# Attention of a fused kernel: transposes, values and outputs an iteration later, GpSimd's work in another order

## The chip, the core and the metric

One core of a Trainium2 chip runs the whole program. The metric is the device time of one execution in microseconds (us). The engines are TensorE (PE in the rows, PEld for its weight loads), VectorE (DVE), ScalarE (ACT), GpSimd (POOL) and SyncE (SP), which here issues every transfer (DMA). Each engine takes its own instructions strictly in the order in which they were written; semaphores make one wait for another.

## What is computed

Local attention with block summaries, then two gated layers. For 16 heads (2 batches of 8), 768 positions and 64 channels, a row sees the positions nearer than 16 and, as 24 further keys, the maxima of `k` over blocks of 32; their values are the block means of `v`:

```python
k_sum = k.reshape(B, H, nb, block, D).max(axis=3)
v_sum = v.reshape(B, H, nb, block, D).mean(axis=3)
scores_l = scale * np.matmul(q, k.transpose(0, 1, 3, 2))
scores_s = scale * np.einsum('bhsd,bhnd->bhsn', q, k_sum) + np.log(block)
a = softmax over [scores_l where |i - j| < 16, scores_s]
x = (a @ concat(v, v_sum)) as 1536 tokens x 512
x = (h * cos(h)) @ w_out            with h = x @ w_in       (2048 wide)
x = (h * tanh(softplus(h))) @ w2_out  with h = x @ w2_in    (2048 wide)
```

Inputs are float32 or, for the weights, float64 that is read as pairs of words and narrowed on the chip.

## The kernel before

The attention goes over 24 steps. A step is a pair of heads and a third of its positions: pair n has the steps 3n, 3n + 1 and 3n + 2. Iteration i of the loop in `attention` works on several steps at once: it computes the scores of step i, the softmax of step i - 1, the transposes of the probabilities of step i - 2 (`probsT`, from `pn` by products with `ident`, copied from PSUM to `pt`), the value products of step i - 3 (`pv`), and the outputs of step i - 4 (`evac`: a rounded high part `xh` by ScalarE and the rest `xl` by VectorE). Beside them it prepares pairs to come: `k` and `q` are transposed on TensorE; ScalarE copies `k` into `kx`; VectorE takes the block maxima `ks` and scales `q` into `qt`; GpSimd copies `qt` into the two halves of `qb`. A softmax step is a row maximum `mx` on VectorE, four exponentials `pb` on ScalarE with their sums, sum and reciprocal `rs` on VectorE, and the multiply `pn` on GpSimd (the phase "norm").

The functions don't issue instructions at once. Each puts them into a named phase with `at(phase, ...)`, and `flush()` at the end of an iteration writes them out phase by phase in the order of the tuple `ORDER`. So `ORDER` sets what stands ahead of what on every engine within an iteration. Loads (`load`, `load_v`, `load_vb`) are written when `plan(i, ...)` comes to them, ahead of everything that `flush` writes; the transfers of the phase "misc" are written last.

The block means of `v` come in two ways. For a pair n with 2n < `MADE` they are made on TensorE: `prep_vm` multiplies the pair's values by a matrix `means`, twelve products into a bank, and ScalarE copies the result into `vm`. For the other pairs GpSimd adds up 32 rows in `block_sums` over a tile `vb` (two groups of `HPG` heads), scales the sums into `vs`, and SP moves them from `vs` to `vm` by small transfers; GpSimd then copies the first half of `vm` to a third place. In both ways `prep_vs` sends `vm` into the value tile `vw` of the pair by two transfers (`vw<-vm`), and the pair's value products need them. There are three value tiles, two of each of `kn`, `qn`, `vm`.

Between the attention's instructions stands the start of the weights: at given iterations `wload` fetches a chunk of `w_in`, `wnarrow` turns it to float32 (one op on ScalarE, three on VectorE: L131, L135, L138, L141) and `wsplit` makes a high and a low part (ScalarE L149, GpSimd L152). In the last iterations the first three blocks of up-projection products (`up`, L188) stand in the phase "fill". After the loop `layers` runs the two gated layers; its first gate begins with L556 on ScalarE and L557 on VectorE.

Of the kernel before, what the change touches and what calls it, by code (L numbers as in the profile page):

```python
# [21 lines left out]
def kernel(  # L22
# [11 lines left out]
    nc = tc.nc  # L34
# [18 lines left out]
    GAP = NB // 2  # L53
# [139 lines left out]
    HPG = 5  # L193
# [4 lines left out]
    def attention(filler):  # L198
        with ExitStack() as es:
# [49 lines left out]
            def build_means():  # L249

                nc.gpsimd.memset(means, 1.0 / BLK)
                for pattern, base, step in (
# [9 lines left out]
            ORDER = ("sc", "xh", "sums", "max", "tr", "tp", "ev", "qev", "pv", "pth", "fill", "qbd", "kmax", "rec", "exp",  # L262
                     "xl", "norm", "gap", "misc")
            todo = {o: [] for o in ORDER}

            def at(phase, fn, *a, **kw):
                todo[phase].append(lambda: fn(*a, **kw))  # L267
# [45 lines left out]
            def prep_vm(n):  # L313
                vm = VM[n] = p2.tile([GAP, 3, 2, D], F32, tag="vm", name="vm")
                if 2 * n >= MADE:
                    for e in range(2):
                        i = 2 * n + e - MADE
                        src = VS[i // HPG][NB * (i % HPG):NB * (i % HPG) + NB]
                        for h in range(2):
                            at("misc", nc.sync.dma_start, out=vm[:, h, e, :], in_=src[GAP * h:GAP * h + GAP])  # L320
                    at("misc", nc.gpsimd.tensor_copy, vm[:, 2], vm[:, 0])
                    return
# [71 lines left out]
            plan(0, prep_vm, 0)  # L394
            plan(1, prep_vs, 0)
# [9 lines left out]
            for n in range(1, NP):  # L405
                plan(3 * n + 1 if 2 * n < MADE else 3 * n, prep_vm, n)
                plan(3 * n + 2 if 2 * n < MADE else 3 * n + 1, prep_vs, n)
                if n > 2:
                    plan(3 * n - 3, load_v, n)
            for g in range(2):  # L410
                plan((2, 9)[g], load_vb, g)
                for c in range(9):
                    plan((4, 11)[g] + c // 2, block_sums, g, c)
# [99 lines left out]
            for i in range(NS + 5):  # L513
                if i >= 4 and i - 4 < NS:
                    evac(i - 4)
# [4 lines left out]
                if 2 <= i < NS + 2:  # L520
                    probsT(i - 2)
                for f in PREP.get(i, ()):
                    f()
                if 3 <= i < NS + 3:
                    pv(i - 3)
# [374 lines left out]
    NS = len(STEPS)  # L900
# [5 lines left out]
    for c, (t0, t1) in enumerate(((7, 10), (9, 12), (13, 16), (15, 18))):  # L906
        at_step(t0, wload, 0, 0, c)
        for part in range(4):
            at_step(t1 + part // 2, wnarrow, 0, 0, c, part)
        at_step(t1 + 2, wsplit, 0, 0, c)  # L910
    at_step(19, wload, 0, 0, 4)
    at_step(21, wload, 0, 0, 5)
# [39 lines left out]
```

## Time and profile before

| what | us |
|---|---|
| median of 3 runs | 654.89 (653.13 to 655.21) |
| the profiled execution | 655.26, its span 653.5 |
| TensorE busy in the span | 616.2 (94%) |
| VectorE busy | 500.9 (77%) |
| ScalarE busy | 333.5 (51%) |
| GpSimd busy | 86.1 (13%) |

The span is the time from the first to the last instruction. The engines' shares are means over parts with different limits: the attention takes the first fifth of the span, the two layers the rest. A row of the timeline shows the start, the duration, engine and line, the operation with output <- inputs and shapes, the number of instructions merged into the row, and in brackets how long the engine was idle before it and what ended that. L267 is the line on which the phases are recorded, so the attention's instructions all carry it and are told apart by their tiles.

### The profile page before, as it was taken

What the parts mean: (1) busy time and instruction counts of PE and PEld (TensorE: products, weight loads), DVE (VectorE), ACT (ScalarE), POOL (GpSimd) and SP (SyncE); (2) the same over time, 40 slices, a digit from 0 to 9 for tenths busy, and PEclk for the clock granted to TensorE, in tenths of its full rate; (3) what the DMA queues carried; (4) which work ended last, traced back from release to release, by engine and by line L of the source; (5) the groups of instructions that cost most, each with busy time, mean ns of one, the idle gap of its engine ahead of it and who ended that gap; (6) DMA issues with size and microseconds to landing.
All of it is one profiled execution on the core that took longest, in us unless ns stands there. A gap on an engine that the chain in (4) does not pass through costs nothing.

```text
span 653.5 us, 8522 instructions
## 1 busy us (share of the span) xinstructions
PE 616.2 (94%) x3004; PEld 515.2 (79%) x3004; DVE 500.9 (77%) x879; ACT 333.5 (51%) x733; POOL 86.1 (13%) x165
## 2 busy tenths in 40 slices
PE   7894877986999999999999999999999999999997
PEld 6784766864888888888888888888888888888886
DVE  4466666398778988888888986977888888888653
ACT  3575676575555644444445545654344444444230
POOL 5483766100000000000000223000000000000000
PEclk9998788997999999999999999999999999999999
DMA  9896844012112212212121210212122222120004
GB/s 186 169 176 151 165 100 107 6 65 96 65 66 96 98 65 65 65 64 66 64 65 66 64 33 0 66 64 66 65 64 65 64 66 81 49 96 33 2 16 178
DMA packets 58665, 51.26 MB, mean 78 GB/s; under 512 B 45326, under 2 KB 46734, under 8 KB 58382
## 3 DMA queue, kind: packets, MB, share of 16 engines
q1 hardware_dynamic: 58622, 50.71, 28.2%
q8 instruction: 24, 0.39, 0.3%
q14 instruction: 19, 0.16, 0.1%
HBM read 46.31 MB, written 3.15 MB: 76 GB/s over the span
## 4 chain that ended last, share of the span: by engine, by line
PE 83%; DVE 6%; POOL 3%; DMA 3%; issue 1%; ACT 1%; SPq 1%; POOLq 0%; ACTq 0%; DVEq 0%
PE bank L709 20%; PE bank L580 20%; PE bank L694 19%; PE bank L188 18%; PE bank L267 7%; POOL pn L267 1%; DMA vb<-in_v_dram 1%; DMA vm<-vs 1%; DVE wx L138 1%; POOL qb L267 1%; DVE wx L141 1%; DVE r L558 1%; POOL ws L152 1%; DVE r L557 1%; DMA vw<-in_v_dram 1%
## 5 line engine op out<-in xcount | busy, mean ns | idle before, releaser
L580 PE MATMUL bank<-gh,ws 128*128 128x512 f32 x384 | 126.7, 392 | 4.9 <-ACT ws L149 4.2
L188 PE MATMUL bank<-xh,ws 128*128 128x512 f32 x384 | 128.1, 395 | 2.0 <-DVE gg L564 1.9
L709 PE MATMUL bank<-ws,gh 128*128 128x512 f32 (+1 forms) x388 | 118.4, 387 | 0.0
L694 PE MATMUL bank<-xh,ws 128*128 128x512 f32 x272 | 91.1, 389 | 0.0
L580 PEld LDWEIGHTS bank<-gh,ws 128*128 128x128 f32 x384 | 72.3, 188 | 21.7 <-ACT ws L149 4.9
L188 PEld LDWEIGHTS bank<-xh,ws 128*128 128x128 f32 x384 | 73.1, 190 | 18.5 <-DVE gg L564 3.3
L709 PEld LDWEIGHTS bank<-ws,gh 128*128 128x128 f32 x388 | 72.6, 188 | 14.8
L556 ACT ACTIVATE n<-bank,b_quarter 128x512 int32<-128x512 f32 x48 | 32.9, 686 | 87.6 <-PE bank L188 87.6
L188 PE MATMUL bank<-xl,ws 128*128 128x512 f32 x192 | 75.6, 394 | 0.0
L709 PE MATMUL bank<-ws,gl 128*128 128x512 f32 (+1 forms) x194 | 75.0, 387 | 0.0
L580 PE MATMUL bank<-gl,ws 128*128 128x512 f32 x192 | 74.9, 390 | 0.0
L149 ACT CAST ws<-wx 128x512 fp32r<-128x512 f32 x64 | 39.6, 620 | 51.5 <-DVE wx L141 51.5
L694 PEld LDWEIGHTS bank<-xh,ws 128*128 128x128 f32 x272 | 51.1, 188 | 10.6
L665 DVE TENSOR_TENSOR gl<-gg,gh 128x512 fp32r<-128x512 f32 x48 | 34.0, 707 | 30.2 <-ACT gh L664 30.2
L721 DVE TENSOR_TENSOR acc<-acc,bank 128x512 f32<-128x512 f32 (+1 forms) x71 | 47.4, 673 | 8.5 <-PE bank L709 8.5
L557 DVE SCALAR_TENSOR_TENSOR r<-n,bank 128x512 f32<-128x512 int32 x48 | 32.8, 684 | 27.2 <-ACT n L556 27.2
L694 PE MATMUL bank<-xl,ws 128*128 128x512 f32 x136 | 52.9, 389 | 0.0
L595 POOL TENSOR_TENSOR xl<-acc,xh 128x512 fp32r<-128x512 f32 x10 | 14.0, 1416 | 261.4 <-ACT xh L593 261.4
L138 DVE SCALAR_TENSOR_TENSOR wx<-wst,wx 128x512 int32<-128x512 int32 x64 | 45.6, 712 | 2.2
L141 DVE SCALAR_TENSOR_TENSOR wx<-wst,wx 128x512 int32<-128x512 int32 x64 | 44.4, 694 | 1.8
L152 DVE TENSOR_TENSOR ws<-wx,ws 128x512 fp32r<-128x512 f32 x60 | 42.1, 703 | 4.8 <-ACT ws L149 4.1
L671 ACT ACTIVATE gg<-gg 128x512 f32<-128x512 f32 x28 | 17.7, 633 | 51.2 <-DVE gg L670 51.2
(110 smaller groups left out, 1062.2 us busy)
## 6 DMA issues: line engine op xcount, KB each, us to landing
wst<-in_moe_w_in_dram SPq DMA_DIRECT2D x32, 512.0 KB
wst<-in_moe_w_out_dram SPq DMA_DIRECT2D x32, 512.0 KB
kn<-in_k_dram SPq DMA_DIRECT2D x16, 192.0 KB
qn<-in_q_dram SPq DMA_DIRECT2D x16, 192.0 KB
vw<-in_v_dram SPq DMA_DIRECT2D x16, 192.0 KB
out_dram<-acc SPq DMA_DIRECT2D x11, 256.0 KB
vb<-in_v_dram SPq DMA_DIRECT2D x2, 960.0 KB
vw<-in_v_dram SPq DMA_DIRECT2D x32, 41.2 KB
```

Source lines behind the costliest of these rows:

```text
L138: nc.vector.scalar_tensor_tensor(out=xi, in0=word[:, :, 0], scalar=29, in1=xi, op0=ALU.logical_shift_right, op1=ALU.bitwise_or)
L141: nc.vector.scalar_tensor_tensor(out=xi, in0=word[:, :, 1], scalar=-2 ** 31, in1=xi, op0=ALU.bitwise_and, op1=ALU.bitwise_or)
L149: nc.scalar.copy(hi, x)
L152: eng.tensor_tensor(out=lo, in0=x, in1=hi.bitcast(F32), op=ALU.subtract)
L188: nc.tensor.matmul(ps, lhsT=SLOT[4 * (g % 2) + a][:, 512 * c + 128 * f:512 * c + 128 * f + 128], rhs=X[e][:, c, TB * j:TB * j + TB], start ...
L267: todo[phase].append(lambda: fn(*a, **kw))
L557: nc.vector.scalar_tensor_tensor(out=r, in0=n, scalar=-C1, in1=h, op0=ALU.mult, op1=ALU.add)
L580: nc.tensor.matmul(ps, lhsT=x, rhs=y, start=(n == 0), stop=(n == len(mm) - 1))
L665: later.append(lambda: nc.vector.tensor_tensor(out=lo, in0=g, in1=hi.bitcast(F32), op=ALU.subtract))
L694: nc.tensor.matmul(ps, lhsT=u, rhs=v, start=start and n == 0, stop=stop and n == len(mm) - 1)
L709: nc.tensor.matmul(ps, lhsT=x, rhs=y, start=(n == 0 and (h == 0 or not stay)), stop=(n == len(mm) - 1 and (h == NH - 1 or not stay)))
L721: nc.vector.tensor_tensor(out=acc, in0=acc, in1=ps, op=ALU.add)
```

## The change

Transposes, values and outputs of a step come one iteration later (i - 3, i - 4, i - 5), and the loop's last iteration now has work. `ORDER` is another: the reciprocals ("rec") come right behind the maxima and the evictions, and the multiply ("norm") ahead of the copies into `qb`, of the weights' part and of the sums, which now come last but two. `HPG` is 4 instead of 5, so that four pairs instead of three have their means from products, and the groups of sums have 96 rows instead of 120. The third part of `vm` comes by transfers, six in place of four, not by a copy on GpSimd. The means of pair 0 are made in iterations 2 and 3 instead of 0 and 1; values are loaded one iteration later; `vb` is loaded at 1 and 12 instead of 2 and 9 and its sums spread over more iterations; the first weight chunks come one or two iterations later.

```diff
-    HPG = 5
+    HPG = 4
...
-            ORDER = ("sc", "xh", "sums", "max", "tr", "tp", "ev", "qev", "pv", "pth", "fill", "qbd", "kmax", "rec", "exp",
-                     "xl", "norm", "gap", "misc")
+            ORDER = ("sc", "xh", "max", "tr", "tp", "ev", "rec", "pth", "pv", "qev", "norm", "kmax", "qbd", "fill", "exp",
+                     "xl", "sums", "gap", "misc")
...
-                        for h in range(2):
-                            at("misc", nc.sync.dma_start, out=vm[:, h, e, :], in_=src[GAP * h:GAP * h + GAP])
-                    at("misc", nc.gpsimd.tensor_copy, vm[:, 2], vm[:, 0])
+                        for h in range(3):
+                            r0 = GAP * (h % 2)
+                            at("misc", nc.sync.dma_start, out=vm[:, h, e, :], in_=src[r0:r0 + GAP])
...
-            plan(0, prep_vm, 0)
-            plan(1, prep_vs, 0)
+            plan(2, prep_vm, 0)
+            plan(3, prep_vs, 0)
...
-                    plan(3 * n - 3, load_v, n)
-            for g in range(2):
-                plan((2, 9)[g], load_vb, g)
-                for c in range(9):
-                    plan((4, 11)[g] + c // 2, block_sums, g, c)
+                    plan(3 * n - 2, load_v, n)
+            for g, at0, steps in ((0, 1, (4, 5, 6, 7, 8, 9, 10, 10, 11)), (1, 12, (14, 14, 15, 15, 16, 16, 17, 17, 18))):
+                plan(at0, load_vb, g)
+                for c, i in enumerate(steps):
+                    plan(i, block_sums, g, c)
...
-                if i >= 4 and i - 4 < NS:
-                    evac(i - 4)
+                if 5 <= i < NS + 5:
+                    evac(i - 5)
...
-                if 2 <= i < NS + 2:
-                    probsT(i - 2)
+                if 3 <= i < NS + 3:
+                    probsT(i - 3)
...
-                if 3 <= i < NS + 3:
-                    pv(i - 3)
+                if 4 <= i < NS + 4:
+                    pv(i - 4)
...
-    for c, (t0, t1) in enumerate(((7, 10), (9, 12), (13, 16), (15, 18))):
+    for c, (t0, t1) in enumerate(((8, 12), (10, 14), (15, 17), (17, 19))):
...
-        at_step(t1 + 2, wsplit, 0, 0, c)
-    at_step(19, wload, 0, 0, 4)
-    at_step(21, wload, 0, 0, 5)
+        at_step(t1 + 3, wsplit, 0, 0, c)
+    at_step(20, wload, 0, 0, 4)
+    at_step(22, wload, 0, 0, 5)
```

SP, at the end of the loads of the first three pairs: before, the two transfers of pair 0's means into its value tile (`vw0<-vm`) stand ahead of the sums' rows `vb` and of pair 3's `kn` and `qn`.

```order
L291 DMA vw2_110<-in_v_dram 15x11x64
L267 DMA vw0_108<-vm_262 12x6x256 x2
L300 DMA vb_366<-in_v_dram 120x2048
L280 DMA kn_419<-in_k_dram 128x6x64 x2
L280 DMA qn_422<-in_q_dram 128x6x64 x2
L280 DMA kn_538<-in_k_dram 128x6x64 x2
```

The same place now:

```order
L291 DMA vw2_110<-in_v_dram 15x11x64
L300 DMA vb_307<-in_v_dram 96x2048
L280 DMA kn_411<-in_k_dram 128x6x64 x2
L280 DMA qn_414<-in_q_dram 128x6x64 x2
L267 DMA vw0_108<-vm_350 12x6x256 x2
L280 DMA kn_523<-in_k_dram 128x6x64 x2
```

The pair of transfers has moved past five others.

GpSimd, two iterations in the middle with sums over `vb` and the weights' subtraction (`ws`, L152): before, the multiply `pn` comes last of these in its iteration.

```order
L267 TENSOR_TENSOR vb_764<-vb_764 120x256 x2
L152 TENSOR_TENSOR ws1_84<-wx_838,ws0_83 128x512
L267 COPY qb1_107<-qt_914 64x4x64 x2
L267 TENSOR_TENSOR pn_912<-pb_858,rs_911 128x472
L267 COPY vm_918<-vm_918 12x128
L267 TENSOR_TENSOR vb_764<-vb_764 120x256 x2
L267 COPY qb1_107<-qt_978 64x4x64 x2
L267 TENSOR_TENSOR pn_976<-pb_908,rs_975 128x472
```

Such iterations now:

```order
L267 TENSOR_TENSOR pn_1061<-pb_1006,rs_1060 128x472
L267 COPY qb0_106<-qt_1063 64x4x64 x2
L152 TENSOR_TENSOR ws1_84<-wx_936,ws0_83 128x512
L267 TENSOR_TENSOR vb_905<-vb_905 96x256 x2
L267 TENSOR_TENSOR pn_1121<-pb_1057,rs_1120 128x472
L267 COPY qb0_106<-qt_1123 64x4x64 x2
L267 TENSOR_TENSOR vb_905<-vb_905 96x256 x2
```

The multiply now opens the iteration, and the copy within `vm` is gone.

TensorE, at the end of the attention: before, the last value products (`pt_1518`) stand ahead of the third block of up products (bank 2, L188).

```order
L188 MATMUL bank1_59<-xh_91,ws0_83 128x512
L188 MATMUL bank1_59<-xl_92,ws0_83 128x512
L188 MATMUL bank1_59<-xh_91,ws1_84 128x512
L267 MATMUL bank7_65<-pt_1518,vw1_109 128x128 x4
L188 MATMUL bank2_60<-xh_91,ws0_83 128x512
L188 MATMUL bank2_60<-xl_92,ws0_83 128x512
```

The same place now:

```order
L188 MATMUL bank2_60<-xh_91,ws0_83 128x512
L188 MATMUL bank2_60<-xl_92,ws0_83 128x512
L188 MATMUL bank2_60<-xh_91,ws1_84 128x512
L267 MATMUL bank7_65<-pt_1543,vw1_109 128x128 x4
L188 MATMUL bank3_61<-xh_91,ws0_83 128x512
L188 MATMUL bank3_61<-xl_92,ws0_83 128x512
```

The last value products now stand behind that block.

## Rows read from the trace of the kernel before

**Rows 1.** Busy us (instructions) by stretch; then granted clock, DMA share, GB/s.
```profile
core 0: us, PE busy (x) PEld busy (x) DVE busy (x) ACT busy (x) POOL busy (x), PEclk, DMA share, GB/s
45.80:48.76 2.96, 2.96 (x28) 2.81 (x26) 2.58 (x8) 2.92 (x13) 2.27 (x7) 1.00 0.47 70
...
54.81:67.57 12.76, 4.44 (x28) 3.96 (x25) 5.42 (x15) 4.27 (x19) 4.58 (x11) 0.66 0.68 155
67.57:118.20 50.63, 39.61 (x266) 36.71 (x265) 32.30 (x80) 34.16 (x133) 32.01 (x54) 0.85 0.52 114
...
132.73:156.37 23.64, 16.72 (x64) 11.44 (x62) 23.16 (x39) 16.04 (x26) 0.00 (x0) 0.96 0.27 89
156.37:653.50 497.13, 493.88 (x2173) 408.80 (x2173) 404.46 (x651) 237.09 (x398) 14.01 (x10) 0.99 0.19 64
```

**Rows 2.** Timeline of VectorE: the first gate.
```profile
132.73 0.69 DVE L557 SCALAR_TENSOR_TENSOR r<-n,bank 128x512 f32<-128x512 int32 x1
```

**Rows 3.** Timeline of TensorE in the attention.
```profile
12.59 2.78 PE L267 MATMUL bank<-vw,means 118*12 118x128 f32 x24 [2.07 <-DMA vw<-in_v_dram]
...
24.35 1.15 PE L267 MATMUL bank<-kx,qb 128*128 128x118 f32 x8 [1.61 <-POOL kx L267]
...
31.66 0.65 PE L267 MATMUL bank<-ident,pn 128*118 128x128 f32 x4
...
36.38 0.36 PE L267 MATMUL bank<-mask,msel 67*128 67x472 bf16 x1
...
64.96 1.11 PE L267 MATMUL bank<-ident,pn 128*118 128x128 f32 x4 [8.32 <-POOL pn L267]
65.86 1.91 PE L267 MATMUL bank<-pt,vw 118*128 118x128 f32 x8
67.57 0.60 PE L267 MATMUL bank<-mask,msel 67*128 67x472 bf16 x1
...
118.20 0.36 PE L267 MATMUL bank<-mask,msel 67*128 67x472 bf16 x1
...
121.75 0.65 PE L267 MATMUL bank<-ident,pn 128*118 128x128 f32 x4 [0.95 <-POOL pn L267]
...
125.90 0.60 PE L267 MATMUL bank<-ident,pn 128*118 128x128 f32 x4
...
129.97 1.05 PE L267 MATMUL bank<-pt,vw 118*128 118x128 f32 x8
```

**Rows 4.** Waits from 0 to 160 us: who for whom, total, times, longest.
```profile
PE bank L267 <- POOL pn L267: 19.1, 12, 8.3
```

**Rows 5.** Timeline of GpSimd: the copy within `vm`.
```profile
62.78 0.28 POOL L267 COPY vm<-vm 12x128 f32<-12x128 f32 x1 [9.46 <-DMA vm<-vs]
```

**Rows 6.** Timeline of SP: when transfers are issued, and how long issuing took.
```profile
22.02 1.83 SPq L267 DMA_DIRECT2D vw<-vm  x2
23.91 0.52 SPq L300 DMA_DIRECT2D vb<-in_v_dram  x1
...
25.60 5.72 SPq L280 DMA_DIRECT2D qn<-in_q_dram  x2
...
71.49 3.19 SPq L267 DMA_DIRECT2D vm<-vs  x4
...
75.94 1.74 SPq L267 DMA_DIRECT2D vw<-vm  x2
...
95.89 0.64 SPq L289 DMA_DIRECT2D vw<-in_v_dram  x1
...
99.07 0.41 SPq L291 DMA_DIRECT2D vw<-in_v_dram  x1
```

**Rows 7.** Busy time by stretch as in rows 1, start of the attention.
```profile
28.00:30.00 2.00, 2.00 (x20) 1.69 (x19) 0.98 (x2) 1.19 (x6) 0.97 (x1) 1.00 0.99 205
```

**Rows 8.** Timeline of VectorE: the longest weight instruction of the attention.
```profile
75.71 1.97 DVE L138 SCALAR_TENSOR_TENSOR wx<-wst,wx 128x512 int32<-128x512 int32 x1
```

**Rows 9.** The page's groups by line: busy us, mean ns, idle us before them.
```profile
L138 DVE SCALAR_TENSOR_TENSOR wx<-wst,wx 128x512 int32<-128x512 int32 x64 | 45.6, 712 | 2.2
```

## Prediction

> **What bounds the kernel now.** I read the busy time by stretches first [rows 1]. From 156.37 to the end TensorE is busy 493.88 of 497.13 us, and the change touches nothing there. From 132.73 to 156.37 VectorE is busy 23.16 of 23.64 us (first gates and weights): this piece can only be moved as a whole. What is left is the attention, which ends for VectorE at 132.73, when the first gate starts [rows 2]. I call iteration i the turn of the loop that computes the scores of step i, and take the start of its mask product as its start.
>
> One iteration at its best is the first of rows 1: 2.96 us, TensorE busy throughout and ScalarE 2.92. From iteration 12 (67.57) to iteration 23 (118.20) [rows 3] eleven iterations take 50.63 us, 4.60 each, and there ScalarE is busy 34.16, VectorE 32.30, GpSimd 32.01, at most 3.1 an iteration; TensorE is at 39.61 only because its granted clock is 0.85, a mixture of the levels 1.2 and 2.4 GHz. So nobody is full: they wait for each other. The list of waits says for whom: TensorE stood 19.1 us for `pn`, GpSimd's multiply [rows 4]. The longest is 8.32 us ahead of 64.96 [rows 3]: GpSimd stood 9.46 us at its copy of `vm` [rows 5], which waits for transfers of `vm` behind the loads, and everything behind that copy, `qb` and `pn`, stood with it. After it the value products take 1.91 instead of 1.05 us (the row at 65.86 against that at 129.97 [rows 3]): TensorE had idled, and the mean granted clock of the stretch from 54.81 is 0.66 [rows 1].
>
> **The change part by part.** The profiled run is 655.26 us with a span of 653.50; the median of three is 654.89, so the two agree within 0.4 and I forecast against 655.26.
>
> *Start, to iteration 6.* The twelve mean products of pair 0 leave the place where TensorE waited 2.07 us for the first values [rows 3]; that alone buys nothing, since the loads decide. The two transfers `vw<-vm` of pair 0 now stand on SP behind `vb`, `kn` and `qn` of pair 3, where before they stood ahead of `vb`. SP issued them at 22.02 and `vb` at 23.91 [rows 6]; now `vb` can go at 22.0. In that queue then lie `vb` 0.79 MB, `kn` and `qn` 0.79, `vw<-vm` 0.15, together 1.73 MB. At the 205 GB/s of the row from 28.00 [rows 7] that is 8.4 us; with about 2 us from a small transfer's issue to its use (the last of four `vm` issues starts some 0.8 us before they end at 74.68, and the transfer that needs it goes at 75.94 [rows 6]) the means land at about 32.5, bounds 31 and 35; I take 33, since the second `qn` was held on SP until 31.32 (25.60 + 5.72 [rows 6]) and the copies queue behind it. The value product of step 0 needs them. TensorE is there at 27 or so: it ended the same work at 31.66, out of which come the waits of 2.07 and 1.61 [rows 3] and one value product (0.9). So it stands some 5.5 us, and as after 64.96 the clock is low after it: from 64.96 to 67.57 transposes and values took 2.61 us [rows 3], twice their usual 1.3, and the scores behind them were slow too: about 2 us lost. Step 0's product, iteration 5 (2.0 at half speed for its scores, 2.0 for the rest) put iteration 6 at 33 + 1.8 + 4.1 = 38.9, against 36.38 [rows 3]: 2.5 us later than before.
>
> *Iterations 6 to 12.* Six iterations at 3.0 (2.96 in rows 1) and two groups of mean products: pair 2's as before, and pair 3's, which is new. A group is 24 instructions at 12.59, 2.78 us [rows 3]; nothing hides it, since TensorE is full here. ScalarE's two copies lie under it. That is 18 + 5.5 = 23.5, so iteration 12 starts at 62.4. Before, it started at 67.57, with the stall of 8.32 and the low clock inside. The stall goes: GpSimd's copies of `vm` are gone (a third transfer does it), and pair 3, for which it waited, needs no `vm` transfer. What is late next on this stretch: the values of pair 3, issued in iteration 7 and needed in iteration 10; nine microseconds for 0.47 MB, enough. Gain at iteration 12: 5.2 us.
>
> *Iterations 12 to 23.* The transposes take the multiply of an iteration earlier, and the multiply stands first on GpSimd, ahead of `qb`, the weight subtraction and the sums; reciprocals stand right behind the maxima on VectorE. So `pn` has a whole iteration to be late in. GpSimd's own load is 2.9 an iteration on the mean [rows 1]; iterations 14 to 17 hold more, which that iteration absorbs. The reciprocal now stands ahead of `qt` and `ks` and waits for ScalarE's exponentials; behind it wait GpSimd's copies, used three iterations later. The price of an iteration lies between 3.1 (ScalarE never idle, 34.16 / 11) and 4.60 (nothing gained). I take 3.5, nearer to the floor, as the same loop without weights ran at 2.96. 11 x 3.5 = 38.5: iteration 23 starts at 100.9, not 118.20. This gives 12.1 us.
>
> *Drain.* The pipeline is one iteration longer, and the third block of up-projection products now stands ahead of the last value product, not behind it. A drain iteration is 125.90 - 121.75 = 4.15 us [rows 3]. Before, from iteration 23's start to the first gate were 14.53 us. Now: scores, transposes and values 2.4, three drain iterations 12.45, and from the last value product to the gate as before 132.73 - 129.97 = 2.76, together 17.6. The earlier up block returns nothing, since VectorE sets the end of the next 23.6 us. Cost: 3.1 us. The first gate starts at 100.9 + 17.6 = 118.5, not 132.73.
>
> *Sum:* -5.2 - 12.1 + 3.1 = -14.2 us; 655.26 - 14.2 = 641.1 us.
>
> **A rule against the change.** One step of VectorE's weight conversion (L138) took 1.97 us with GpSimd at work beside it [rows 8]; the mean of all 64 is 0.71 [rows 9]. The Trainium skill, SBUF — State Buffer, section "SBUF: two separate sides", states that a VectorE instruction with two SBUF inputs and a GpSimd instruction lock each other out for the whole of one. By that rule the multiply, moved right behind the reciprocals, would run into the weight conversion that follows them; the trace agrees that such collisions occur. By it the sum would be 651.2 us, by the mean row it is 641.1. The mechanism stands below, from rows, as the third rival.
>
> **The rivals.**
> 1. *The start does not stall and the loop reaches its floor.* For it: the loads of the start have the same bytes less 0.2 MB. Against it: the queue. Without the stall iteration 6 comes 6 us earlier, as far as `kn` of pair 3 allows; with 3.25 an iteration 2.7 more: 632.4.
> 2. *SP becomes the pace.* A pair whose means come from sums now issues six `vm` transfers instead of four (3.19 for four [rows 6], so 4.8), two `vw<-vm` 1.74, six value loads 3.6 (95.89 to the last's start at 99.07 and its 0.41 [rows 6]), two pairs of loads about 2 and a weight: 12.5 us, 4.1 an iteration. Against it: `vw<-vm` has three iterations of lead. If SP sets it, 11 x 4.1 = 45.1, 6.6 more than the forecast: 647.7.
> 3. *VectorE and GpSimd collide.* Four weight chunks meet the multiply in two iterations each; at 1.97 - 0.71 = 1.26 us a collision [rows 8, 9], all on the path, 10.1: 651.2. For it the long row; against it that VectorE's load of 2.9 an iteration [rows 1] leaves room under 3.5.
> 4. *It doesn't do what it says:* TensorE no longer waits for `pn` but for something else as long, the exponentials behind the maxima; iterations stay at 4.60: 641.1 + 12.1 = 653.2.
> 5. *Slower: late means.* Every `vw<-vm` of pairs 4 to 7 stands behind six `vm` transfers and six loads in one queue, as pair 0's does behind `vb`, and a value product waits for each. A wait like that at the start costs 5.5 + 2 = 7.5 us. Two of them eat the gain; three give 641.1 + 22.5 = 663.6. Against it: the queue is at 114 GB/s in that stretch [rows 1], half of its best.
>
> **How the numbers follow.** Forecast 0.55 (own range 634 to 646.5: a front 3 us better or worse, 3.2 to 3.8 an iteration); rival 1 0.14; rival 2 0.10; rival 3 0.05; rival 4 0.08; rival 5 0.08. About 0.3%, 2 us, is what a measurement of this kernel can tell from no change. Rival 4 lies within it; rival 5 is slower; the rest, 0.84, is faster. The range goes from rival 1 to rival 3, 631 to 652, and leaves out 0.16 above and some of rival 1 below.
>
> **What would show it.** Right: the next copy of `vm` on GpSimd is not there; TensorE's waits for `pn` shrink from 19.1 to under 3 us; iteration 12 near 62, 23 near 101, the first gate near 118.5; the granted clock from 12 to 23 near 1. One stall of about 5 us for `vw<-vm` near 28 to 33. Wrong: a loop still at 4 us or more an iteration, with TensorE waiting for `vw<-vm` (rivals 2 and 5) or VectorE's weight rows at 1.3 us and more (3).

## The result, and the profile of the changed kernel

| | before | changed |
|---|---|---|
| median, us | 654.64 (4 runs, 653.13 to 655.21) | 648.21 (4 runs, 647.99 to 648.40) |
| profiled run, its span | 655.26, 653.5 | 648.26, 646.6 |
| iterations 6, 12, 23 start at | 36.38, 67.57, 118.20 | 39.08, 61.93, 107.63 |
| first gate | 132.73 | 127.22 |

The ratio is 0.9905, 95% interval 0.9888 to 0.9922: faster by 6.4 us (0.95%), where the forecast was 14.2. Busy time by stretches, as in [rows 1]: iterations 6 to 12, 12 to 23, the drain, the stretch behind the first gate, the rest; then the drain's first 4.37 us.

```profile
core 0: us, PE busy (x) PEld busy (x) DVE busy (x) ACT busy (x) POOL busy (x), PEclk, DMA share, GB/s
39.08:61.93 22.85, 22.85 (x200) 21.24 (x198) 15.03 (x43) 17.75 (x77) 15.98 (x32) 1.00 0.70 169
61.93:107.63 45.70, 33.14 (x267) 30.95 (x265) 37.19 (x87) 36.82 (x146) 36.06 (x57) 0.97 0.58 130
107.63:127.22 19.59, 19.59 (x111) 17.60 (x110) 6.30 (x17) 8.78 (x26) 1.95 (x2) 0.88 0.14 35
127.22:150.90 23.68, 15.17 (x53) 9.89 (x51) 23.20 (x39) 16.06 (x26) 0.00 (x0) 0.83 0.27 89
150.90:646.60 495.70, 492.55 (x2173) 407.97 (x2173) 404.68 (x651) 237.25 (x398) 14.04 (x10) 1.00 0.19 64
...
107.63:112.00 4.37, 4.37 (x21) 4.31 (x20) 1.73 (x5) 1.86 (x7) 0.80 (x1) 0.50 0.45 133
```

Iterations 6 to 12 are TensorE's: it is busy all the time, at full clock. From 12 to 23 TensorE is idle for 12.56 us. Its timeline there and at the start, as in [rows 3] (the last bracket: idle time ahead, and who is named as having ended it; of the waits from 61.93 on, one of 0.20 in iteration 15 is left out):

```profile
33.63 2.04 PE L267 MATMUL bank<-pt,vw 118*128 118x128 f32 x8 [4.80 <-DMA vw<-vm]
35.46 0.60 PE L267 MATMUL bank<-mask,msel 67*128 67x472 bf16 x1
...
71.10 1.13 PE L267 MATMUL bank<-pt,vw 118*128 118x128 f32 x8 [1.32 <-ACT pt L267]
...
79.29 1.13 PE L267 MATMUL bank<-pt,vw 118*128 118x128 f32 x8 [1.78 <-DMA kn<-in_k_dram]
...
85.04 1.15 PE L267 MATMUL bank<-kx,qb 128*128 128x118 f32 x8 [1.56 <-POOL kx L267]
...
91.78 1.13 PE L267 MATMUL bank<-pt,vw 118*128 118x128 f32 x8 [1.87 <-DVE rs L267]
...
95.22 1.13 PE L267 MATMUL bank<-pt,vw 118*128 118x128 f32 x8 [0.57 <-DVE xl L267]
...
99.59 1.13 PE L267 MATMUL bank<-pt,vw 118*128 118x128 f32 x8 [1.71 <-DVE xl L267]
...
105.79 2.04 PE L267 MATMUL bank<-pt,vw 118*128 118x128 f32 x8 [3.55 <-DMA vw<-vm]
107.63 0.60 PE L267 MATMUL bank<-mask,msel 67*128 67x472 bf16 x1
```

These waits sum to the 12.56; with the 33.14 us that TensorE is busy they make the 45.70. About 0.9 of the busy time is half clock, in the product at 105.79 (2.04 in place of 1.13). No wait for `pn` of [rows 4] is left among them. The last is for the means of pair 6; behind it TensorE goes at half clock until 112 (the 0.50 above). Where those means came from, on GpSimd and on SP (start, us; the first two rows of SP are those of pair 0's means at the start):

```profile
92.61 0.37 POOL L267 TENSOR_SCALAR vs<-vb 96x64 f32<-96x64 f32 x1
```
```profile
24.10 3.99 SPq L280 DMA_DIRECT2D qn<-in_q_dram  x2
28.20 1.84 SPq L267 DMA_DIRECT2D vw<-vm  x2
...
78.43 4.60 SPq L267 DMA_DIRECT2D vm<-vs  x6
...
87.51 1.76 SPq L267 DMA_DIRECT2D vw<-vm  x2
89.39 0.44 SPq L113 DMA_DIRECT2D wst<-in_moe_w_in_dram  x1
93.00 4.62 SPq L267 DMA_DIRECT2D vm<-vs  x6
97.72 0.67 SPq L289 DMA_DIRECT2D vw<-in_v_dram  x1
...
101.40 1.76 SPq L267 DMA_DIRECT2D vw<-vm  x2
```

SP stood 3.2 us from 89.83 until the sums of group 1 were done at 92.98, then issued six `vm` transfers, six loads and the two `vw<-vm`, the second until 103.16; the product follows 2.6 us behind. The wait of 1.87 us at 91.78 is named for VectorE's `rs`, but the second `vw<-vm` of pair 5 was issued until 89.27, 2.5 us before: it is the same kind of wait, for late means (run e22 below names it so).

Two other waits are named for what did not end them. The value products alternate between two banks, so those of an iteration need the `xl` of the iteration before, and VectorE does that last, behind the weight conversion:

```profile
68.27 1.12 DVE L138 SCALAR_TENSOR_TENSOR wx<-wst,wx 128x512 int32<-128x512 int32 x1
69.42 0.77 DVE L141 SCALAR_TENSOR_TENSOR wx<-wst,wx 128x512 int32<-128x512 int32 x1
70.11 0.85 DVE L267 TENSOR_TENSOR xl<-bank,xh 64x256 fp32r<-64x256 f32 x2
...
78.34 0.85 DVE L267 TENSOR_TENSOR xl<-bank,xh 64x256 fp32r<-64x256 f32 x2
```

These `xl` end at 70.96 and 79.19, 0.14 and 0.10 us ahead of the products at 71.10 and 79.29; the `pt` that the first needs was copied an iteration earlier, and the keys in the name of the second are no operand of it. So of the 12.56 us the waits for `xl` are 5.58 (0.20, 0.57, 1.71, 1.32 and 1.78), those for late means 5.42 (1.87 and 3.55), and one for `kx` is 1.56.

Behind the first gate the changed kernel's profiled run took 519.4 us, the kernel before 520.8 and the other runs below 519.6 to 521.2. The change touches nothing there; in the 36.34 us that begin 23.66 behind the gate the granted clock is 0.97 where it was 0.93. So 1.4 of the 6.4 us are not the change's doing as far as the runs show, and a difference of 1 to 2 us between two kernels at the first gate can be gone in the time.

### The profile page after: what moved, and what is told of

It is laid out like the page before. It is cut to its first block, busy times and chain, and to the rows that moved or that the text cites. A ratio compares the mean times of both kernels' runs of the same rounds, so it can differ in the third digit from the quotient of the medians.

```text
span 646.6 us, 8555 instructions
## 1 busy us (share of the span) xinstructions
PE 614.8 (95%) x3028; PEld 514.6 (80%) x3028; DVE 504.5 (78%) x879; ACT 333.8 (52%) x735; POOL 86.8 (13%) x160
## 4 chain that ended last, share of the span: by engine, by line
PE 87%; DVE 6%; ACT 3%; DMA 2%; issue 1%; POOL 1%; SPq 1%; ACTq 0%; DVEq 0%; POOLq 0%
PE bank L709 20%; PE bank L580 20%; PE bank L694 19%; PE bank L188 19%; PE bank L267 9%; DMA vw<-vm 1%; ACT pb L267 1%; DVE r L558 1%; DVE wx L138 1%; DVE r L557 1%; DMA wst<-in_moe_w_in_dram 1%; DVE wx L141 1%; ACT xh L267 0%; DVE gg L564 0%; ACT pt L267 0%
## 5 line engine op out<-in xcount | busy, mean ns | idle before, releaser
L188 PE MATMUL bank<-xh,ws 128*128 128x512 f32 x384 | 128.3, 395 | 3.6 <-DVE gg L564 3.5
L188 PEld LDWEIGHTS bank<-xh,ws 128*128 128x128 f32 x384 | 72.9, 190 | 20.2 <-DVE gg L564 5.2
L188 PE MATMUL bank<-xl,ws 128*128 128x512 f32 x192 | 75.5, 393 | 0.0
L138 DVE SCALAR_TENSOR_TENSOR wx<-wst,wx 128x512 int32<-128x512 int32 x64 | 46.3, 724 | 2.1
L152 DVE TENSOR_TENSOR ws<-wx,ws 128x512 fp32r<-128x512 f32 x60 | 42.1, 703 | 4.7 <-ACT ws L149 4.1
L131 ACT ACTIVATE wx<-wst 128x512 f32<-128x512 f32 x64 | 43.0, 673 | 3.9 <-DMA wst<-in_moe_w_in_dram 3.9
## 6 DMA issues: line engine op xcount, KB each, us to landing
vw<-in_v_dram SPq DMA_DIRECT2D x32, 41.2 KB
```

The source lines that it names most:

```text
L131: nc.scalar.activation(out=x, in_=hf, func=AF.Copy, scale=2.0 ** -112)
L138: nc.vector.scalar_tensor_tensor(out=xi, in0=word[:, :, 0], scalar=29, in1=xi, op0=ALU.logical_shift_right, op1=ALU.bitwise_or)
L152: eng.tensor_tensor(out=lo, in0=x, in1=hi.bitcast(F32), op=ALU.subtract)
L188: nc.tensor.matmul(ps, lhsT=SLOT[4 * (g % 2) + a][:, 512 * c + 128 * f:512 * c + 128 * f + 128], rhs=X[e][:, c, TB * j:TB * j + TB], start ...
```

## The experiments

The expectations name theories of what set the time. A is VectorE's order (`xl` behind the weight conversion). B is collisions of VectorE with GpSimd. C is late means, of pair 6 above all: a value product stands ready and its pair's means are not in `vw` yet; later C is read as SP's queue. D is the stall for pair 0's means at the start. E is that the later products return nothing net. S and G are SP's issuing and GpSimd's sums, each as the last link of C. Times are medians; ratios are to the kernel before, run beside them, with 95% intervals; 0.9888 to 0.9922 is that of the changed kernel. Starts and waits are of the profiled execution.

### Which part of the change gained

**e7**: the kernel before with `HPG = 4`, and

```diff
-for h in range(2):
-    ... in_=src[GAP * h:GAP * h + GAP]
-at("misc", nc.gpsimd.tensor_copy, vm[:, 2], vm[:, 0])
+for h in range(3):
+    ... in_=src[r0:r0 + GAP]        # r0 = GAP * (h % 2)
```

> The kernel before with one part of the change alone: four pairs' means by products, and the third part of `vm` by a transfer in place of GpSimd's copy. If the 8.32 us ahead of 64.96 in [rows 3], GpSimd's wait for the transfers of `vm`, was the whole gain of the change, this kernel has it too, less a group of mean products of 2.78: 649 to 650. If the later transposes and the new orders carry the gain as well, it is at 651 to 653, with TensorE's waits for `pn` still at 8 us or more. If SP's two more issues a pair take it all, it is at 655 or above.

Measured 647.11, ratio 0.9895 (0.988 to 0.991): the whole gain of the change, from its smallest part. (Its two halves, the means of pair 3 by products and the third transfer, were not run apart.) Iteration 6 starts at 35.54, 12 at 61.02, 23 at 110.01, the first gate at 124.52. TensorE still waits for `pn`, mostly about 1 us, in eight of the eleven iterations from 12 to 23; of its waits up to 160 us (total, times, longest):

```profile
PE bank L267 <- POOL pn L267: 12.9, 12, 2.5
```

Against it the rest of the change loses 3.5 us at the start (39.08), gains 2.6 from 6 to 12 (22.85 for 25.48) and 3.3 from 12 to 23 (45.70 for 48.99), and loses 5.1 in the drain (19.59 for 14.51).

**e5**: the changed kernel with the shallower pipeline (`evac(i - 4)`, `probsT(i - 2)`, `pv(i - 3)`). Step 0's value product then stands ahead of pair 0's means and is computed without them.

> The changed kernel with transposes, value products and outputs an iteration earlier again, as before the change; everything else of it stays (orders, means of pair 3 by products, places of the sums and loads). The kernel before with one part of the change alone (four pairs by products, no copy of `vm`) took 647.11, all of the gain. Theory E, that the later products return nothing net: they cost about 5 us in the drain (19.6 from iteration 23 to the first gate instead of 14.5) and give back about as much between iterations 12 and 23; then this kernel is at 646 to 649, with waits for `pn` of 6 us or more between iterations 12 and 23 and a drain near 14.5. My forecast's reading, that the iteration of slack is what shortens 12 to 23: 651 to 654. If the new orders alone already take the waits for `pn` away: 643 to 644.

Measured 649.31, ratio 0.9919 (0.9904 to 0.9934): E holds for the time, but not by its mechanism. The drain is 14.52, yet there is one wait for `pn` in all. What came instead are three late means (the first is named for L138, but it too comes 2.8 us behind SP's second `vw<-vm`, issued until 75.07):

```profile
77.86 1.92 PE L267 MATMUL bank<-pt,vw 118*128 118x128 f32 x8 [3.56 <-DVE wx L138]
...
91.77 2.05 PE L267 MATMUL bank<-pt,vw 118*128 118x128 f32 x8 [3.08 <-DMA vw<-vm]
...
107.51 2.05 PE L267 MATMUL bank<-pt,vw 118*128 118x128 f32 x8 [5.64 <-DMA vw<-vm]
```
```profile
PE bank L267 <- POOL pn L267: 1.0, 1, 1.0
```

So in this kernel the new orders take the waits for `pn` away without the added iteration (some may lie hidden under the late means; e14 below has 3.8 us of them). What the added iteration hides is late means: 12.3 us here, 5.4 in the changed kernel.

**e6**: the changed kernel with the `ORDER` line of before.

> The changed kernel with the order of an iteration's work on each engine as before: GpSimd's multiply last, behind `qb`, the weight subtraction and the sums, the reciprocals behind VectorE's weight conversion, the sums first on GpSimd. With the multiply an iteration ahead of its transposes, its place within the iteration should matter little: 647 to 650, with waits for `pn` under 3 us. It may gain, since the sums, first on GpSimd now, end earlier and the means of pair 6 with them (`vs` before 92): 645 to 646. If the new order was needed as well, waits for `pn` come back at 5 us or more: 652 or above.

Measured 645.28, ratio 0.9851 (0.9831 to 0.9871): 3 us faster than the change, with no wait for `pn` over 0.5 us. So the added iteration alone is enough against those waits as well. The profiled execution is the fastest of four, 642.35; in it 12 to 23 takes 42.88, where e7, with the old orders and without the added iteration, took 48.99, and the drain 18.17 for 14.51. The two kernels also differ in the places of loads and sums, so this does not price the iteration alone.

### What set iterations 12 to 23

**e1**: `"qbd", "xl", "fill", "exp"` for `"qbd", "fill", "exp", "xl"`.

> The changed kernel with one word moved: VectorE's subtraction `xl` stands ahead of the weight conversion in the order of an iteration, not behind it. Theory A, VectorE's order sets the middle (the value banks alternate, so a value product waits for the `xl` of the iteration before, which is VectorE's last work there): TensorE's waits for `xl` of 0.20, 1.78, 0.57 and 1.71 us ahead of value products go, iteration 23 starts near 103.5 instead of 107.63, and the time falls by 3 to 5 us to about 644. Theory B, VectorE and GpSimd collide, and it is the longer instructions that cost: VectorE has the same work, 37.19 us of 45.70, L138 stays at 1.1 to 1.45 us in the iterations with weights, and the time stays at 648 within 1.5. Theory C, the late means of pair 6 set it: the 3.55 us wait in iteration 22 only grows by what is gained before it, and the time stays at 648 within 1.

Measured 646.71, ratio 0.9891 (0.9871 to 0.991). Iteration 14 fell from 4.41 to 2.85 and the waits for `xl` went, 5.58 us in all, but iteration 23 starts at 106.25, only 1.4 earlier. Late means stand in their place: 2.35 us for pair 5 and 4.22 for pair 6 in place of 1.87 and 3.55, and 1.36 for pair 4, which had lain under the wait for `xl` (two of the three have another name in the trace; each product stands 2.5 to 2.7 us behind its second `vw<-vm`).

```profile
104.41 2.05 PE L267 MATMUL bank<-pt,vw 118*128 118x128 f32 x8 [4.22 <-DMA vw<-vm]
```

A is right on the wait and wrong on its worth; the interval overlaps that of the changed kernel.

**e2**: `plan(3 * n - 2 + (n == 7), load_v, n)`.

> The changed kernel with the six loads of pair 7's values one iteration later, so that on SP the two transfers of the means of pair 6 stand ahead of them. Theory C, the late means of pair 6: the loads took SP from 97.72 to 101.35, so the transfers go some 3.7 us earlier, the 3.55 us wait ahead of a value product in iteration 22 goes, and the half clock behind it too: iteration 22 at about 3.5 instead of 7.08 us, the drain at 18 to 19 instead of 19.59, the time at 643 to 644.5. Theories A and B (VectorE in the middle, or its collisions with GpSimd): iterations 14 to 21 stay as they are, and the wait turns into one of VectorE's in iteration 22 (1.7 us as in 21): the time at 646 to 647.

Measured 649.12, ratio 0.993 (0.9908 to 0.9952). Iteration 22 took 3.53 as C expected; the means of pair 7, now behind those loads, were late in the drain instead:

```profile
116.61 2.04 PE L267 MATMUL bank<-pt,vw 118*128 118x128 f32 x8 [3.59 <-DMA vw<-vm]
```

The time is not told apart from the changed kernel's. In this queue another order alone only chose who waits.

**e3**: `plan(0, prep_vm, 0)`, `plan(1, prep_vs, 0)`.

> The changed kernel with the means of pair 0 back in iterations 0 and 1, their place before the change, so that their two transfers stand on SP ahead of `vb`. Theory D, the stall at 28.8 to 33.6 (4.80 us for `vw<-vm`) and the slow clock behind it cost what they look like: iteration 6 starts at 35 to 36.5 instead of 39.08, and the time falls by 2.5 to 4 to about 645. Rival: the loads that now go later (`vb`, keys and queries of pair 3) or the middle take it back, and iteration 12 starts at 61 to 62 as it does now (61.93): the time stays within 1 of 648.

Measured 645.07, ratio 0.9865 (0.9848 to 0.9882). Iteration 6 starts at 35.67, 12 at 58.52, 3.4 us earlier, and this is kept: D holds. But the transfers do not stand ahead of `vb`, as the expectation has it:

```profile
21.67 0.40 SPq L300 DMA_DIRECT2D vb<-in_v_dram  x1
22.17 1.86 SPq L267 DMA_DIRECT2D vw<-vm  x2
```

What they passed are pair 3's keys and queries, at whose `qn` SP stood until 28.09 in the changed kernel.

**e4**: in `wnarrow`, for the first four chunks, parts 1 to 3 (VectorE's three steps) issue nothing, so these weights are wrong.

> The changed kernel without VectorE's three conversion steps of the first four weight chunks (L135, L138, L141, twelve instructions in iterations 12 to 20): these weights are then wrong, and so is the output; it prices the work. Theories A and B together: these twelve take 10.8 us of VectorE's 37.19 there (6.9 at their usual durations, 3.9 more from collisions with GpSimd); without them the waits for `xl` (4.3 us) and for the reciprocals (1.87) go and iterations 14 to 21 take 2.9 to 3.4 each: iteration 23 near 100 and the time at 640 to 642. Theory C alone: iterations shorten but pair 6's means, which hang on GpSimd's sums and SP, come no earlier than now: iteration 23 at 105 or later, the time at 646 to 648.

Measured 644.31, ratio 0.9847 (0.9831 to 0.9863), 3.9 us for 11.1 us less work on VectorE: between what A with B and what C alone expected. Iterations 14 and 15 take 2.85, but 16, 19 and 22, one a pair, take 6.35, 6.00 and 5.05. TensorE's waits there:

```profile
77.51 2.03 PE L271 MATMUL bank<-pt,vw 118*128 118x128 f32 x8 [2.41 <-DMA vw<-vm]
...
90.55 1.47 PE L271 MATMUL bank<-pt,vw 118*128 118x128 f32 x8 [2.61 <-DVE xl L271]
...
102.28 1.13 PE L271 MATMUL bank<-pt,vw 118*128 118x128 f32 x8 [2.39 <-DMA vw<-vm]
```

Without VectorE's load the means of pairs 4, 5 and 6 are late. The wait of 2.61 is named for `xl`, but that `xl` frees the bank of the next iteration's products; the product stands 2.4 us behind the second `vw<-vm` of pair 5 (issued until 88.15), as the others stand 2.8 and 2.6 behind theirs.

### SP's issues or GpSimd's sums

**e9**: `for h in range(2)` for the `vm` transfers of pairs 4 to 7; both `vw<-vm` then read the same two parts, and the second row of means is wrong.

> The changed kernel with four `vm` transfers a pair instead of six for pairs 4 to 7: the third part of `vm` is left out, and the second row of means of these pairs then holds its halves in the wrong order, so the output is wrong; it prices SP. Theory C, now: SP's queue is the pace from pair 4 on. In the changed kernel its second `vw<-vm` of pairs 4, 5 and 6 ends at 75.10, 89.27 and 103.16, 14 us a pair, and a value product starts 2.5 to 2.6 us behind the last two (91.78 and 105.79). Two transfers less are 1.5 us a pair: pair 6's ends near 101.6, its product starts near 104.2, and the time falls by 1.5 to 3, to 645.3 to 646.8. Theory A (VectorE's `xl`): nothing of it changes before iteration 22, and the time stays at 647.5 to 648.5, or gains the 1.5 of the last wait alone.

Measured 647.56, ratio 0.9897 (0.988 to 0.9913): within the changed kernel's interval. Pair 5's `vw<-vm` went 2.9 us earlier, but SP then waited 3.5 us longer for `vs`; pair 6's product still waited 3.80. 12 to 23 took 44.29, 1.4 less, about the 1.5 a pair that C counted; in the time it does not show.

**e20**: `(nc.gpsimd if n >= 3 else nc.sync).dma_start` for L290 and L291.

> The changed kernel, whole, with the four small value loads of a pair (the edges of the blocks, L290 and L291) issued by GpSimd instead of SP for pairs 3 to 7. They took SP 2.1 us a pair (0.65 + 0.40, twice). Theory S, SP's issuing is the pace: in the changed kernel SP issues for 13.08 us of the 14.17 between its last `vw<-vm` of pair 4 and that of pair 5. Then pair 5's means come 2 us earlier and the wait of 1.87 us in iteration 19 goes; pair 6's come 2 us earlier too, since only two of its six value loads stand between `vm` and `vw<-vm`: 644 to 646. Theory G, GpSimd's sums are the pace (SP stood 3.2 us for `vs` of pair 6): GpSimd gets work on top, `vs` comes no earlier than 92.98 or later, and the time is 648 to 651.

Measured 648.07, ratio 0.9908 (0.9894 to 0.9921): no gain. SP was freed, GpSimd paid, and `vs` of group 1 was done 2.2 us later than in the changed kernel (95.18): its groups of these issues between 60 and 108 us, and TensorE's longest wait there:

```profile
L290 POOL DMA_DIRECT2D vw<-in_v_dram x6 | 3.8, 631 | 0.2 <-issue 0.2
L291 POOL DMA_DIRECT2D vw<-in_v_dram x6 | 3.6, 604 | 0.0
```
```profile
87.44 1.66 PE L267 MATMUL bank<-kx,qb 128*128 128x118 f32 x8 [4.22 <-POOL kx L267]
```

**e22**: `"sums"` third in `ORDER`.

> The changed kernel with one word moved: GpSimd's sums stand first in its iteration, as before the change, with the multiply behind them as the change has it. Theory G, the sums of group 1 are the last link (their end at 92.98 released SP): they end about an iteration earlier, before 90, pair 6's second `vw<-vm` ends near 98 to 100 instead of 103.16, its wait of 3.55 us falls under 1, and the time is 645 to 646, as with all the old orders (645.28). If the multiply, now behind the sums, holds TensorE: 648 or more. If what gained in that run was the start (iteration 6 at 36.25 instead of 39.08), it is seen there: the stall of 4.80 us shrinks here too or it does not.

Measured 643.3, ratio 0.9845 (0.9821 to 0.9869): one word is worth 4.9 us. The start gave nothing (iteration 6 at 39.60, a stall of 5.23). `vs` was done at 90.50, 2.5 us earlier; the wait for pair 6 fell to 1.80, not under 1 as G expected, and the product behind it kept the full clock (1.13); the wait of 1.56 for `kx` fell to 0.18; 12 to 23 took 41.92 and the drain 18.0:

```profile
91.49 1.13 PE L267 MATMUL bank<-pt,vw 118*128 118x128 f32 x8 [1.88 <-DMA vw<-vm]
...
103.40 1.13 PE L267 MATMUL bank<-pt,vw 118*128 118x128 f32 x8 [1.80 <-DMA vw<-vm]
```

**e10**: `block_sums` and `load_vb` left out, `VS` set to zero at the start.

> The changed kernel without GpSimd's block sums and without the two loads of `vb` for them; the means of pairs 4 to 7 are zeros set at the start, so the output is wrong. GpSimd loses some 12 us of work, SP the 3.2 us that it stood for `vs` at 89.83, and the first queue 0.79 MB ahead of the means of pair 0. Theory C: the start gains 2 to 4 us (the transfers of pair 0's means land earlier), SP's transfers for pairs 5 and 6 are no longer held, the waits at 91.78 and 105.79 fall under 1 us, and iteration 12 to iteration 23 takes about 40 us instead of 45.70: the time at 638 to 641. Theory B (collisions): VectorE's L138 and L141 fall back to 0.7 us where a sum stood beside them, at most 2 us. Theory A: the waits for `xl` stay, 12 to 23 takes 43 to 44, and the time is 643 to 644.

Measured 634.26, ratio 0.9702 (0.9684 to 0.9719): beyond what any theory expected. 5.8 us are at the start (iteration 6 at 33.27), where `vb` no longer stands ahead of pair 0's means, 6.1 from 12 to 23 (39.61). It prices the sums with their loads, not their place.

**e11**: the sums of group 1 in iterations 12 to 16, `plan({4: 10, 5: 12, 6: 17, 7: 18}.get(n, 3 * n + 1), prep_vm, n)` and `{4: 12, 5: 14, 6: 18, 7: 20}` for `prep_vs`.

> The changed kernel, whole, with only the means of pairs 4 to 7 earlier: group 0's sums end in iteration 9 and not 11, the second `vb` is loaded in iteration 10 and not 12, its sums stand in iterations 12 to 16 and not 14 to 18, and the `vm` and `vw<-vm` transfers of pairs 4, 5, 6, 7 go in iterations 10/12, 12/14, 17/18, 18/20 and not 12/13, 15/16, 18/19, 21/22. SP has the same work, begun while it has room. Theory C: no value product of pairs 4 to 7 waits for `vw<-vm`, iteration 22 takes 3.5 instead of 7.08, the half clock behind it goes, and the time is 642.5 to 644.5. Theory A: the wait becomes one for `xl`; 645.5 to 647. Against both: GpSimd's sums now stand in iterations 12 and 13, and loads of pairs 4 and 5 behind `vm` transfers, which could make an iteration there wait (4 us in place of 2.85): 648 or more.

Measured 645.47, ratio 0.987 (0.9853 to 0.9888). Iteration 22 takes 2.42; iteration 13 takes 6.75, since `vw<-vm` of pair 3 now stood behind the `vm` of pair 4, and its product waited 2.79. Both sides of the expectation came true.

### The edits together

**e13**: e1, e3, and e11 with 4: 11, 5: 13 and 4: 13, 5: 15.

> The changed kernel, whole, with the three edits that each gained alone: the means of pair 0 in iterations 0 and 1 (645.07), VectorE's `xl` ahead of the weight conversion (646.71), and the means of pairs 4 to 7 earlier (645.47), the last with the `vm` transfers of pairs 4 and 5 one iteration later than there, since in that run the transfers of pair 3's means stood behind them and a value product in iteration 13 waited 2.79 us. If the three waits stand one behind the other (theories A, C and D together), the gains add up, 3.1 + 1.5 + 2.7 us and the 3 us of iteration 13: iteration 6 near 35.5, 12 near 58.4, 23 near 95.5, the first gate near 114.5, the time 636 to 639. If each only uncovers the next, as the late means took back most of what `xl` gained: 641 to 643.

Measured 640.48, ratio 0.9778 (0.9765 to 0.9791). Iteration 12 at 58.80, 23 at 99.41. The longest that is left is one iteration of 7.84 us, in which the keys of pair 7 come late:

```profile
70.83 4.57 SPq L267 DMA_DIRECT2D vm<-vs  x6
75.51 1.04 SPq L280 DMA_DIRECT2D kn<-in_k_dram  x2
```
```profile
79.51 0.66 PE L267 MATMUL bank<-ident,kn 128*128 128x128 f32 x2 [2.17 <-DVE qt L267]
```

**e14**: e13 with e5's depth.

> The kernel of the three edits together, with transposes, value products and outputs an iteration earlier again, as before the change. It prices the iteration of slack where no means are late. Theory E (it returns nothing net): same time as the three edits within 2 us, the drain 5 us shorter and 12 to 23 about 5 us longer, with TensorE's waits for `pn` back. If the slack is worth more once the means are in time, this kernel is 4 us or more slower than the three edits; if the new orders already suffice, it is 3 to 5 us faster.

Measured 646.17, ratio 0.9866 (0.9849 to 0.9883): 5.7 us slower. 4.6 of it stand at iteration 12 (63.43), from the start, where pair 0's means are waited for again (1.98); 12 to 23 takes 41.58 for 40.61; the drain, with 2.90 for pair 7's means in it, 19.25. So here the added iteration is worth more than its drain, again mostly for transfers; `pn` costs 3.8 us in five waits.

**e15**: e13 with two `vm` transfers a head, and in `prep_vs` `at("exp", nc.scalar.copy, VM[n][:, 2], VM[n][:, 0])`.

> The kernel of the three edits together (640.48) with the third part of `vm` of pairs 4 to 7 copied by ScalarE, an iteration after the four transfers, instead of by two more transfers: two issues a pair less on SP, 1.5 us of about 12.5. In that kernel SP issues without a break from 58.1 to 104, and the keys and queries of pair 7 (issued at 75.51 behind 4.57 us of `vm` transfers) and a weight behind them come late: TensorE waits 0.96 and 2.17 us in iteration 17, ScalarE 1.63 and VectorE 2.73 for the weight. Theory S: keys and queries land 3 us earlier (two pairs' savings), the waits and the half clock behind them (iteration 17 takes 7.83 us) go: 635.5 to 638. Theory G: 640 within 1. Against both: ScalarE's copy waits for the transfers and holds its exponentials: 642 or more.

Measured 638.67, ratio 0.9766 (0.9747 to 0.9785). The interval overlaps that of e13. In the profile the keys' wait and the half clock are gone:

```profile
60.55:98.75 38.20, 33.05 (x268) 30.00 (x265) 35.51 (x86) 34.92 (x141) 32.23 (x53) 1.00 0.67 145
```

Two more on e13: the edge loads from GpSimd (e16) gave 641.88, ratio 0.9815 (0.9795 to 0.9836), no gain where 635 to 638 was expected if SP alone were the pace; all old orders but `xl` (e17) gave 640.97, 0.9797 (0.9777 to 0.9816), the same. That fits the reading that in e6 they gained through the earlier sums, which e22 shows by themselves.

**e21**: e15, with the old `ORDER` in iterations 0 to 5.

> The kernel of the three edits with ScalarE's copy (638.67), with the old orders in iterations 0 to 5 and those of the change from 6 on. In the profiled runs of the three edits iteration 6 starts at 35.94 with the new orders and at 33.85 with the old ones, while 12 to 23 takes 40.61 and 42.08. If both differences are of the orders, this has the better of each: 636 to 637. If the start differs by the first loads alone (iteration 1 starts at 15.44 and 15.04, and at 17.19 in the profiled run of ScalarE's copy), it stays at 638 to 639.

Measured 637.85, ratio 0.975 (0.9726 to 0.9773). Iteration 6 starts at 35.70, no earlier than in e13: not told apart from e15. Both beat the changed kernel by about 10 us.

## Why the prediction was right and wrong

*Start.* Right: the stall for pair 0's means was 4.80 (5.5 forecast), half clock behind it, iteration 6 at 39.08 (38.9). e3 confirms the price, and e10 gives 5.8 us without `vb`.

*Iterations 6 to 12.* Right: 22.85 (23.5), iteration 12 at 61.93 (62.4). `vm`'s copy and the stall of 8.32 are gone. (The 0.47 MB for a pair's values is 0.56, two loads of 192 KB and four of 41.2; nothing hung on it.)

*Iterations 12 to 23.* This step failed: 11 x 3.5 = 38.5 was forecast, 45.70 came, 7.2 more; with 0.5 won at iteration 12, 2.0 lost in the drain and 1.4 won behind the gate it is the whole miss. The step that failed is the 3.5 us an iteration: mean loads of at most 3.1 were taken as if an iteration's slack could average them out, and the three iterations of lead of `vw<-vm` and the room that VectorE has on the mean were taken to cover the rest. What was said of `pn` came true, but the slack did not reach two other links, and these cost 5.42 and 5.58 us. The means of pairs 5 and 6 were 1.87 and 3.55 late: the sums, which now stand behind almost everything on GpSimd, were done at 92.98, two iterations of TensorE behind the one in which they are written, and SP issues for 13.08 us of the 14.17 between pair 4's and pair 5's last `vw<-vm`. And `xl`, VectorE's last work of an iteration, releases a value bank that TensorE needs in the next. The rest is 1.56 for `kx` and the half clock. What comes late next was looked for only in the stretch to 12. The sign that the prediction named for being wrong is what came: 4.15 us an iteration, with waits for `vw<-vm`.

*Drain.* The term of 17.6 assumed full clock; 19.59 came, 4.37 of it at 0.50, which is 2.2 us. e22, where the clock held, took 18.0. Behind the gate the run is 1.4 us shorter than before, which nobody forecast; without this luck the gain would be 5.0.

*The rivals.* Rival 2 (647.7) has the measured time and part of the mechanism: SP is nearly full, but relieving SP alone (e9) gains 1.4 us from 12 to 23 and no time while the sums are late, and e20 loads GpSimd with what it takes from SP. e22 and e11 show that earlier sums gain. With `xl` earlier and SP relieved as well (e15), the forecast's 38.5 is reached, at 38.20 in the profile, though its time is not told apart from e13's. How much of the wait is SP's and how much the sums' was not separated: each frees what the other then fills. Rival 5's waits came, but at 1.87 and 3.55 rather than 7.5. Rival 4 had the form right: no wait for `pn` is left and others stand in its place, though at 4.15 an iteration, not 4.60. Rival 3: four L138 took 1.19 on the mean in the changed kernel from 39.08 to 107.63, beside 0.71 [rows 9], and all twelve weight steps there 11.1 us, some 4 more than at their shortest (0.43, 0.69, 0.69). That is 0.48 a step of L138, far below the 1.26 a collision of that rival. The Trainium skill, SBUF — State Buffer, section "SBUF: two separate sides", states that a VectorE instruction with two SBUF inputs and a GpSimd instruction that reads SBUF block each other for the whole of one. The longer steps fit that in kind, but no run here took away the collisions alone. e4 took away work and collisions together, so the collisions' own share stays open.

*Where the gain came from.* The means of pair 3 by products and the third transfer, without the rest, have all of it (e7). The rest of the change gains 5.9 us from iteration 6 to 23 and loses 8.6 at the start and in the drain. That multiplies a whole iteration early gain from 12 to 23 was not shown: where depth alone was put back (e5), the waits that came were for means, and `pn` had one of 1.0.

## What to carry to other kernels

Before adding a pipeline stage, list for each operand of the delayed step who delivers it: slack for one operand is worth little when another has less. Here the stage by itself gained nothing told apart in the changed kernel (e5) and 5.7 us once the means were earlier (e14 against e13), mostly by hiding transfers. A queue that issues in order and is filled nine tenths is an engine of the loop and belongs in the sum with its waits, not only its issues. For each engine ask also where in the iteration the result that another needs is made, not only how long the engine is busy: `xl` cost 5.58 us of waits as the last work of an engine that was not full. A cure of one wait uncovers the next, so try cures together too (e1 alone 1.5 us, e13 7.7). And try each part of a change alone: here one part held all of the gain, and the place of one word in the orders another 4.9 us.

## What the runs showed of the hardware

- A transfer of 3 KB held SP no shorter than one of 192 KB: 0.77 us for 12 x 64 elements (six `vm` in 4.60 to 4.62), 0.64 to 0.67 for a load of 64 x 12 x 64. The edge loads held SP 0.64 and 0.41 us, and GpSimd, when it issued them (e20), 0.63 and 0.60.
- The price of a wait through the clock is not told by its length alone: in e4 two waits for `vw<-vm` were 2.41 and 2.39 us long, and the eight products behind them took 2.03 us, at half clock, and 1.13, at full. This part of a stall's price has to be read from the rows behind it.
- The name that the profile gives a wait was wrong where the DMA was last (91.78; 77.86 in e5; 90.55 in e4; 79.51 in e13) and, the other way, where `xl` was last (71.10 and 79.29). From the end of a pair's second `vw<-vm` issue to a product that waited for it passed 2.3 to 3.0 us in the loop and the drain (more at the start, behind large loads: 3.6 in the changed kernel); that and the ends of the `xl` rows tell which of the two it was.
